# Own output tiles for the second batch in the last stage of a three-stage kernel, the last one stored in two halves

## The chip, the cores and the metric

One Trainium2 chip; the program runs on 1 core. The metric is the device time of one execution in microseconds (us). The engines are named as the profile names them: PE is TensorE's matmul, PEld its weight load, DVE VectorE, ACT ScalarE, POOL GpSimd, SP SyncE, whose queue issues the DMAs of this stage. TensorE's granted clock is 1.00 at 2.4 GHz and 0.50 at 1.2 GHz.

## The reference, cut to what matters

Three layers follow one another: an attention with bucketed masks, a mixture of experts in which every token goes to one expert, and a mixture of attention heads. The last one is what the change touches (two batches, S = 768 rows, D = 512 columns, E = 4 experts, Hd = 64):

```
logits = x @ w_gate                        # top 2 of 4 experts, softmax over the two
for e in range(E):
    q, k, v = x @ wq[e], x @ wk[e], x @ wv[e]
    scores = scale * (q @ k.T), causal mask, softmax -> a
    ye = a @ v @ wo[e]
    out += w[token, e] * ye                # w is 0 for an expert that was not chosen
```

## The kernel before

The kernel has three stages; the last is the class StageC. It takes two experts together as a unit u = (b, pp) with b the batch and pp the pair, so there are four units, and it cuts the 768 rows into halves h of 384 and into six tiles i of 128 (tile i belongs to half i // 3). For each unit it projects q and k, takes scores, exponentials and the causal mask, sums with the values (av), and divides and gates (gate, recip, norm).

The end of the stage is what matters here. norm(u, h, c0, c1) multiplies the gated sum by the reciprocal on DVE into a PSUM tile (can, line 1311), copies that with rounding on ACT (cah, or cxh for the last unit, line 1318), and takes the rest on DVE (cal or cxl, line 1319). For the last unit (1, 1) this is done for one row tile at a time. outp(b, i) then multiplies row tile i with the output weights: six matmuls of 512 columns into one PSUM tile cop (lines 1328 to 1330, three for each pair), then a copy out of PSUM and a DMA of 256 KB to the output (line 1342). For b = 0 the copy is one ACT instruction of 128x512 into a tile cos with two buffers (line 1341). For b = 1 it is an ACT instruction on the first 256 columns (line 1338) and a DVE instruction on the other 256 (line 1339).

Where the copy of b = 1 goes: self.ot is a tile of 2064 columns, a new one (tag w000h or w000l) whenever i is 0 or 3, and a row tile takes the part i % 3 of whichever self.ot is the latest. In the order below outp(1, 3) comes second, so that (1, 1) and (1, 4) both write the second part of the tile w000l, and (1, 2) and (1, 5) both its third part.

The order of all steps is written out by hand (ORDER_C), and each engine takes its instructions in that order; the costs and dependences in plan() give the list of steps and are only checked against it. The order ends, with the units' names left out where they are (1, 1): norm h=1 c=0; outp(1, 0); recip h=0 c=2; recip h=1 c=1; outp(0, 4); outp(1, 3); norm h=0 c=1; outp(0, 0); norm h=1 c=1; recip h=1 c=2; outp(1, 1); outp(1, 4); norm h=0 c=2; outp(0, 1); norm h=1 c=2; outp(1, 2); outp(1, 5). So outp(1, 1) needs norm h=0 c=1, outp(1, 4) needs norm h=1 c=1, outp(1, 2) needs norm h=0 c=2 and outp(1, 5) needs norm h=1 c=2.

The PSUM tiles can and cop (and others) share one ring of three buffers, in the order in which they are asked for:

```
def misc(self, shape, nm):
    return self.ps.tile(shape, F32, name=nm, tag="misc", bufs=3)
```

Counted along the order, cop of outp(1, 1) takes the buffer of can of norm h=0 c=1, and cop of outp(1, 2) that of can of norm h=0 c=2. The first matmul of a group so waits for the DVE instruction at line 1319 of that norm.

The tiles cu0, cu1, ck0, ck1, cq0 and cq1 hold what qk, low, twice, qcopy and mrow make of one unit (U, K and Q of its two experts), each with two buffers that the four units take in turn; their last readers are the score matmuls at lines 1256 and 1257. One more pair of instructions bears on the argument: low (line 1198, DVE) subtracts from partitions 64 to 127 of a PSUM tile cqp into the tile cl, and twice (line 1203, ACT) then copies the same partitions of that PSUM tile into another place (ck, partitions 0 to 63), so that the second needs no result of the first.

Of the kernel before, what the change touches and what calls it, by code (L numbers as in the profile page):

```python
# [8 lines left out]
F32 = mybir.dt.float32  # L9
# [8 lines left out]
B, H, S, D = 2, 8, 768, 64  # L18
DM = H * D
NP = H // 2  # L20
NKT = S // 128
# [11 lines left out]
WN = 2064  # L33
# [994 lines left out]
class StageC:  # L1028
# [292 lines left out]
    def outp(self, b, i):  # L1321
        nc = self.nc
        wh, wl = (a[:, 1040:2064].rearrange("p (k n) -> p k n", k=2) for a in self.wt[1])
        p = self.misc([128, DM], "cop")
        c = slice(128 * i, 128 * i + 128)
        for pp in range(2):
            ah, al = self.o[b, pp]
            nc.tensor.matmul(p, ah[:, c], wh[:, pp, :], start=pp == 0, stop=False)  # L1328
            nc.tensor.matmul(p, ah[:, c], wl[:, pp, :], start=False, stop=False)
            nc.tensor.matmul(p, al[:, c], wh[:, pp, :], start=False, stop=pp == 1)  # L1330
        if b == 0:
            t = self.p.tile([128, DM], F32, name="cos", bufs=2)
        else:
            if i % 3 == 0:
                self.ot = self.rp.tile([128, WN], F32, name="cot", tag=f"w000{'hl'[i // 3]}")
            t = self.ot[:, DM * (i % 3):DM * (i % 3) + DM]
        if b:
            nc.scalar.copy(t[:, :DM // 2], p[:, :DM // 2])
            nc.vector.tensor_copy(t[:, DM // 2:], p[:, DM // 2:])
        else:  # L1340
            nc.scalar.copy(t, p)
        nc.sync.dma_start(self.out[b, c], t)

    def plan(self):
        pl = Plan(dict(misc=3, sc=3, av=2))
# [4 lines left out]
        def add(name, *a, ops, deps=(), **kw):  # L1350
            pl.add((name, *a), lambda: getattr(self, name)(*a), ops, deps, **kw)
# [5 lines left out]
        for b in range(B):  # L1357
            for i in T:
                dep = [("trans", 0, j) for j in range(i // 3 * 3, i // 3 * 3 + 3)] if b else []
                if b:  # L1360
                    add("gather", b, i, ops=[("Pool", 1255)], deps=dep + [("busy",)], tail=2400)
                else:
                    add("came", b, i, ops=[(None, 1400 + 1255 * i)])
                add("scale", b, i, ops=[("ACT", 620) if b or i % 2 else ("DVE", 430, "p")], deps=[("gather" if b else "came", b, i)])
                dep = [("qk", u, x, i // 3) for u in us[:2] for x in X] + [("vproj", 0, i)] if b else []
                add("trans", b, i, ops=[("PE", 438 + (0 if b or i > 1 else (872, 436)[i])), ("ACT", 480), ("DVE", 605)], deps=[("scale", b, i)] + dep, bank="misc")
                add("vproj", b, i, ops=[("PE", 1440), ("ACT", 330)], deps=[("trans", b, i)], bank="misc")
                add("outp", b, i, ops=[("PE", 1390)] + ([("ACT", 290), ("DVE", 330)] if b else [("ACT", 490)]) + [("SP", 500)],
                    deps=[("norm", (b, 0), i // 3), ("norm", (1, 1), i // 3, i % 3, i % 3 + 1) if b else ("norm", (0, 1), i // 3)]
                    + ([("outp", b, i - 1)] if b and i % 3 else []), bank="misc", tail=2000)  # L1370
            add("gate1", b, ops=[("DVE", 1300, "p"), ("ACT", 200)], deps=[("vproj", b, i) for i in T])
            add("gate2", b, ops=[("DVE", 600, "p")], deps=[("gate1", b)])
            add("gate3", b, ops=[("PE", 110), ("DVE", 200), ("SP", 2500)], deps=[("gate2", b)] +
                ([("gate", u, h) for u in us[:2] for h in X] if b else []), bank="misc", tail=3500)
        for n, u in enumerate(us):
            b = u[0]
# [206 lines left out]
```

## Time and profile before

| | |
|---|---|
| median of 3 runs | 607.95 us (605.28 to 609.09) |
| the profiled execution | 608.14 us |
| its span, first to last instruction | 606.4 us |
| mean granted clock of TensorE | 0.987 |
| PE busy | 579.6 us (96%) |
| DVE, ACT, POOL busy | 443.1, 369.8, 252.1 us |

The span is what the trace covers; 1.74 us of the profiled execution's time lie outside it. Busy PE counts matmuls whose ends are modelled, so that one matmul is shown running into the next: the distance of their starts tells the pace.

### The profile page before, as it was taken

The page shows a single profiled execution, that of the slowest core. Times are in us where ns is not written, and L with a number is a line of the kernel's source. Part 1 is how long each engine was busy: PE and PEld are TensorE (multiplying, and loading weights), DVE is VectorE, ACT ScalarE, POOL GpSimd, SP SyncE. Part 2 cuts the span into 40 slices and gives each one's busy share as a digit, 9 for nine tenths or more (in the row PEclk, how much of TensorE's full clock was granted, in tenths as well). Part 3 has the DMA queues.
Part 4 walks back from the last instruction along what each step waited for, and adds up shares of the span by engine and source line. Part 5 has one row for each costly group of instructions (what it writes and reads, how often), then busy time and mean ns, then how long its engine had stood idle before and what let it go on. Part 6 is the DMA issues. An engine that isn't in the chain of part 4 may idle for free. (4 is left out here: it accounts for less than half of the span.)

```text
span 606.4 us, 9769 instructions
## 1 busy us (share of the span) xinstructions
PE 579.6 (96%) x3537; PEld 448.8 (74%) x3537; DVE 443.1 (73%) x853; ACT 369.8 (61%) x676; POOL 252.1 (42%) x256
## 2 busy tenths in 40 slices
PE   8999989999899999899999999999989999998995
PEld 3556657767576675798898998997969878787573
DVE  6699888988889798756656776755444576787872
ACT  4999878989695476154545545544537565554541
POOL 7696577686767784620000000000044024653840
PEclk8999999999999999899999999999999999999998
DMA  8535347265425415247656757665555010210222
GB/s 230 206 130 174 119 151 261 75 225 157 166 62 174 120 56 183 89 138 250 242 176 248 243 198 242 220 233 174 177 166 155 18 28 15 66 27 2 54 105 104
DMA packets 53718, 88.81 MB, mean 146 GB/s; under 512 B 3860, under 2 KB 26512, under 8 KB 53408
## 3 DMA queue, kind: packets, MB, share of 16 engines
q1 hardware_dynamic: 51712, 81.78, 41.3%
q0 software_dynamic: 1952, 6.34, 3.3%
q8 instruction: 29, 0.48, 0.4%
q14 instruction: 25, 0.20, 0.1%
HBM read 66.18 MB, written 20.26 MB: 143 GB/s over the span
## 5 line engine op out<-in xcount | busy, mean ns | idle before, releaser
L320 POOL TENSOR_TENSOR acc<-acc,pt 128x768 f32<-128x768 f32 x56 | 110.6, 1977 | 43.0 <-ACT pt L298 40.6
L274 DVE TENSOR_REDUCE m<-mp 128x1 f32<-128x384 f32 x192 | 96.4, 548 | 10.0 <-PE mp L273 9.2
L298 ACT ACTIVATE pt<-sc 128x384 f32<-128x384 f32 x192 | 85.5, 486 | 24.1 <-PE sc L297 21.1
L1079 POOL DMA_INDIRECT xg<-ys,slot x12 | 12.2, 1018 | 193.4 <-DVE wl L1049 185.7
L850 DVE TENSOR_TENSOR wlo<-wraw,whi 128x1024 fp32r<-128x1024 f32 x64 | 76.3, 1231 | 12.3 <-ACT whi L849 12.2
L307 PE MATMUL av<-pt,vt 128*64 128x385 f32 (+1 forms) x384 | 70.7, 493 | 0.0
L273 PE MATMUL mp<-km,qm 128*128 128x384 f32 x192 | 65.3, 379 | 5.4 <-DVE m L274 3.6
L849 ACT ACTIVATE whi<-wraw 128x1024 fp32r<-128x1024 f32 x64 | 64.4, 1053 | 9.0 <-DMA wraw<-in_w_dram 5.3
L295 PE MATMUL sc<-qm,km 128*128 128x384 f32 x192 | 67.6, 352 | 1.2 <-ACT pt L298 0.6
L297 PE MATMUL sc<-q,k 128*128 128x384 f32 x192 | 64.6, 336 | 0.0
L889 PE MATMUL hp<-xth,whi 128*128 128x256 f32 x224 | 63.0, 281 | 1.7 <-PEq L1017 1.7
L890 PE MATMUL hp<-xtl,whi 128*128 128x256 f32 x224 | 62.9, 281 | 0.0
L891 PE MATMUL hp<-xth,wlo 128*128 128x256 f32 x224 | 62.8, 280 | 0.0
L273 PEld LDWEIGHTS mp<-km,qm 128*128 128x128 f32 x192 | 35.6, 192 | 25.1 <-DVE m L274 10.6
L907 PE MATMUL yp<-whi,hh 128*128 128x512 f32 x128 | 51.5, 402 | 0.0
L908 PE MATMUL yp<-wlo,hh 128*128 128x512 f32 x128 | 50.4, 393 | 0.0
L909 PE MATMUL yp<-whi,hl 128*128 128x512 f32 x128 | 50.3, 393 | 0.0
L307 PEld LDWEIGHTS av<-pt,vt 128*64 128x64 f32 x384 | 25.4, 136 | 32.1 <-issue 28.8
L894 ACT ACTIVATE hh<-hp 128x512 fp32r<-128x512 f32 x32 | 19.1, 598 | 45.0 <-PE hp L891 44.9
L1281 POOL TENSOR_TENSOR cp<-cp,cp 128x384 f32<-128x384 f32 (+2 forms) x50 | 39.5, 812 | 17.0 <-PE cav L1273 16.1
L889 PEld LDWEIGHTS hp<-xth,whi 128*128 128x128 f32 x224 | 42.1, 188 | 2.4 <-issue 2.1
L895 DVE SCALAR_TENSOR_TENSOR hl<-hp,hh 128x512 fp32r<-128x512 f32 x32 | 22.0, 688 | 28.4 <-ACT hh L894 28.4
(263 smaller groups left out, 1387.6 us busy)
## 6 DMA issues: line engine op xcount, KB each, us to landing
wraw<-in_w_dram SPq DMA_DIRECT2D x32, 1024.0 KB
xs<-zt SPq DMA_DIRECT2D x13, 512.0 KB
x<-in_k_dram SPq DMA_DIRECT2D x14, 384.0 KB
x<-in_q_dram SPq DMA_DIRECT2D x14, 384.0 KB
xsb<-xs SPq DMA_DIRECT2D x7, 512.0 KB
ys<-ysb SPq DMA_DIRECT2D x7, 512.0 KB
vt<-in_v_dram SPq DMA_DIRECT2D x8, 384.0 KB
xp<-in_q_dram SPq DMA_DIRECT2D x7, 384.0 KB
```

Source lines behind the costliest of these rows:

```text
L273: nc.tensor.matmul(mp, QM[i][:, o:o + 128], KM[i][:, h * S + c * HS:h * S + (c + 1) * HS], start=True, stop=True)
L274: nc.vector.tensor_reduce(s["m"][:, qh, h, t, c:c + 1], mp, axis=AX.X, op=ALU.max)
L295: nc.tensor.matmul(sc, KM[i][:, h * S + kt * 128:h * S + kt * 128 + 128], QM[i][:, (2 * qh + h) * HS:(2 * qh + h + 1) * HS], start=True, s ...
L297: nc.tensor.matmul(sc, K1[i][:, h, ks], Q1[i][:, h, qs], start=False, stop=True)
L298: nc.scalar.activation(PT[(u * 12 + x) % NPB][:, h, :HS], sc, AF.Exp, scale=SCALE)
L307: nc.tensor.matmul(s["av", qh][64 * h:64 * h + 64, :HS + 1 - qh], s["v"][:, h, kt, :], P[:, h, :HS + 1 - qh], start=kt == 0, stop=kt == NK ...
L320: (nc.vector if u == NU - 1 else nc.gpsimd).tensor_add(s["acc", qh], p, P)
L849: nc.scalar.activation(hi[:, s], r[:, s], AF.Copy)
L850: nc.vector.tensor_sub(lo[:, s], r[:, s], hi[:, s].bitcast(F32))
L889: nc.tensor.matmul(p[:, f2, :], hi, xh[:, k, :], start=k == 0, stop=False)
L890: nc.tensor.matmul(p[:, f2, :], hi, xl[:, k, :], start=False, stop=False)
L891: nc.tensor.matmul(p[:, f2, :], lo, xh[:, k, :], start=False, stop=k == 3)
```

## The change

In the second batch each output row tile gets a tile of its own: the tags cu0, cu1, ck0, ck1, cq0 and cq1 are each asked for once more (i = 0 to 5), and the first 512 of their 768 columns are used. For i = 0 to 4 the copy is one ACT instruction of 128x512, as in the first batch. For i = 5 ACT copies the first 256 columns into the own tile and DVE the other 256 into a further tile (tag w000h), and each half has its own store of 128 KB; SP issues them one after the other. The cost entries of plan() follow; the order of the steps is the same. DVE so loses five copies, ACT's five copies are twice as wide, and SP issues one DMA more.

```diff
+        homes = ("cu0", "cu1", "ck0", "ck1", "cq0", "cq1")
         if b == 0:
             t = self.p.tile([128, DM], F32, name="cos", bufs=2)
         else:
-            if i % 3 == 0:
-                self.ot = self.rp.tile([128, WN], F32, name="cot", tag=f"w000{'hl'[i // 3]}")
-            t = self.ot[:, DM * (i % 3):DM * (i % 3) + DM]
-        if b:
-            nc.scalar.copy(t[:, :DM // 2], p[:, :DM // 2])
-            nc.vector.tensor_copy(t[:, DM // 2:], p[:, DM // 2:])
-        else:
+            t = self.p.tile([128, S], F32, name=homes[i], bufs=2)[:, :DM]
+        if b == 0 or i < NKT - 1:
             nc.scalar.copy(t, p)
-        nc.sync.dma_start(self.out[b, c], t)
+            nc.sync.dma_start(self.out[b, c], t)
+            return
+        t2 = self.rp.tile([128, WN], F32, name="cot", tag="w000h")[:, :DM // 2]
+        n = DM // 2
+        nc.scalar.copy(t[:, :n], p[:, :n])
+        nc.vector.tensor_copy(t2, p[:, n:])
+        nc.sync.dma_start(self.out[b, c, :n], t[:, :n])
+        nc.sync.dma_start(self.out[b, c, n:], t2)
...
-                add("outp", b, i, ops=[("PE", 1390)] + ([("ACT", 290), ("DVE", 330)] if b else [("ACT", 490)]) + [("SP", 500)],
+                add("outp", b, i, ops=[("PE", 1390)] + ([("ACT", 290), ("DVE", 330)] if b and i == NKT - 1 else [("ACT", 590)]) + [("SP", 500)],
```

## Rows read from the trace of the kernel before

**Rows 1.** The waits of 575 to 606.4 us: total us, times, longest.
```profile
DVE cot L1339 <- ACT cot L1338: 7.8, 5, 2.5
ACT cot L1338 <- DMA out_dram<-cot: 5.2, 2, 2.6
PE cop L1328 <- DVE cxl L1319: 2.4, 2, 1.9
```

**Rows 2.** The chain that ended last, 580 to 606.4 us: start, us, what.
```profile
593.13 2.01 DMA out_dram<-cot
...
597.46 0.23 PE cop L1329
...
598.32 0.43 PE cop L1329
...
600.07 2.00 DMA out_dram<-cot
...
602.57 0.42 DVE cot L1339
```

**Rows 3.** Timeline, 587 to 591 us, around TensorE's first stop.
```profile
587.13 1.75 DVE L1300 RECIPROCAL cr<-cr 128x128 f32<-128x128 f32 x2
588.05 0.33 SPq L1342 DMA_DIRECT2D out_dram<-cos  x1
588.79 0.37 ACT L1338 COPY cot<-cop 128x256 f32<-128x256 f32 x1 [0.77 <-PE cop L1330]
589.54 0.29 DVE L1311 TENSOR_TENSOR can<-ca,cr 128x128 f32<-128x128 f32 x1
589.74 0.40 PE L1330 MATMUL cop<-wh,cal 128*128 128x512 f32 x1
589.86 0.28 ACT L1318 ACTIVATE cxh<-can 128x128 fp32r<-128x128 f32 x1 [0.70 <-DVE can L1311]
590.61 0.47 PE L1328 MATMUL cop<-wh,cah 128*128 128x512 f32 x1 [0.47 <-DVE cxl L1319]
```

**Rows 4.** Timeline, 593 to 597.5 us, around its second stop.
```profile
593.23 0.40 PE L1330 MATMUL cop<-wh,cxl 128*128 128x512 f32 x1
594.62 0.40 PE L1330 MATMUL cop<-wh,cal 128*128 128x512 f32 x1
595.24 0.37 ACT L1338 COPY cot<-cop 128x256 f32<-128x256 f32 x1 [2.59 <-DMA out_dram<-cot]
595.64 0.42 DVE L1339 COPY cot<-cop 128x256 f32<-128x256 f32 x1 [2.54 <-ACT cot L1338]
596.31 0.28 ACT L1318 ACTIVATE cxh<-can 128x128 fp32r<-128x128 f32 x1 [0.69 <-DVE can L1311]
596.96 0.50 PE L1328 MATMUL cop<-wh,cah 128*128 128x512 f32 x1 [1.95 <-DVE cxl L1319]
597.30 0.39 PE L1329 MATMUL cop<-wl,cah 128*128 128x512 f32 x1
```

**Rows 5.** Busy time by stretch: PE, PEld, DVE, ACT, POOL, PEclk, DMA share, GB/s.
```profile
594.40:597.00 2.60, 0.65 (x4) 0.23 (x2) 1.01 (x4) 1.07 (x3) 0.00 (x0) 1.00 0.12 44
597.80:601.20 3.40, 3.40 (x10) 2.54 (x8) 0.42 (x1) 0.37 (x1) 0.00 (x0) 0.50 0.29 110
603.80:604.00 0.20, 0.00 (x0) 0.00 (x0) 0.00 (x0) 0.00 (x0) 0.00 (x0) 1.00 0.65 246
604.40:604.60 0.20, 0.00 (x0) 0.00 (x0) 0.00 (x0) 0.00 (x0) 0.00 (x0) 1.00 0.74 277
```

**Rows 6.** Timeline, 600.5 to 603 us, the last row tile.
```profile
601.10 0.46 PE L1330 MATMUL cop<-wh,cxl 128*128 128x512 f32 x1
602.17 0.37 ACT L1338 COPY cot<-cop 128x256 f32<-128x256 f32 x1 [2.58 <-DMA out_dram<-cot]
```

**Rows 7.** All instructions of lines 1341, 1342, 1256 and 1257: ns min/median/max, first and last start.
```profile
L1341 ACT COPY cos<-cop x6: 579/586/588, 579.3 to 596.5; 128x512 f32<-128x512 f32 x6
L1342 SPq DMA_DIRECT2D out_dram<-cot x6: 332/332/333, 587.2 to 603.0; - x6
L1256 PE MATMUL csc<-cu,ck x36: 219/344/449, 539.9 to 579.1; 128*128 128x384 f32 x20, 128*128 128x256 f32 x8, 128*128 128x128 f32 x8
L1257 PE MATMUL csc<-cq,cl x36: 273/335/347, 540.2 to 579.2; 65*128 65x384 f32 x20, 65*128 65x256 f32 x8, 65*128 65x128 f32 x8
```

**Rows 8.** Whom ACT waited for at line 1203 (us, times), a copy from PSUM.
```profile
  DVE cl L1198: 5.2, 8
```

## The prediction

> **What bounds the kernel now.** I read the end of the last stage first, since the change touches nothing ahead of it. The list of waits of the last 31 us [rows 1] shows three that belong together: ACT's copies waited 5.2 us for stores of the output tile, in two waits; DVE's copies waited 7.8 us for ACT's copies; and TensorE waited 2.4 us for DVE's rounding rest. The chain that ended last [rows 2] shows how they hang together: it runs twice through the 2.0 us flight of a store of cot. These are the two places at which a part of a tile is written again: outp(1, 4) takes the part that outp(1, 1) has just sent to a store, outp(1, 5) that of outp(1, 2). The reader is to see in the timeline what an ACT copy that waits for a store does to the rest [rows 4]: it begins at 595.24, DVE's half of the copy stands behind it until 595.64, the norm's instructions for the next row tile stand behind that on both engines (cxh at 596.31), and TensorE, whose last group started its last matmul at 594.62, goes on only at 596.96. After this stop its granted clock is 0.50 (1.2 GHz) from 597.8 to 601.2, having been 1.00 in the stretch with the stop [rows 5], and the starts of its matmuls, 0.23 us apart before, are 0.43 apart [rows 2]. A first, shorter stop of TensorE ends at 590.61 [rows 3]. Then the last row tile's copy waits for a store, until 602.17 [rows 6].
>
> **The change, part by part.** I follow TensorE's start times and shift them.
>
> *First stop.* Before, the product of norm h=0 c=1 stood on DVE at 589.54 behind DVE's half of the copy of outp(1, 3), and cxh followed on ACT at 589.86 [rows 3]. Now DVE has only the two reciprocals ahead of that product; they end at 588.88 at the latest, so it is done by 588.88 + 0.29 = 589.17. ACT is the later one: its copy starts at 588.79 as before, but takes 0.59 (the 128x512 copy of line 1341) [rows 7], so cxh begins at 589.38. From cxh to the first matmul it took 590.61 - 589.86 = 0.75 us here and 596.96 - 596.31 = 0.65 us at the second stop [rows 3, 4]; with 0.7 TensorE goes on at 590.08 in place of 590.61. It can't before 589.74 + 0.23 = 589.97. Gain 0.5, bounds 0.3 and 0.64.
>
> *Second stop.* outp(1, 4) starts its last matmul at 593.23 before [rows 4], now at 592.73, and ends it 0.40 later at 593.13. ACT's copy (no store to wait for) takes 593.15 to 593.74, cxh follows, and 0.7 later, at 594.44, outp(1, 2) may start. TensorE would be free for it at 594.62 + 0.23 - 0.5 = 594.35. So 0.1 of the stop is left: ACT's wide copy, queued ahead of cxh, is what is late next, by a hair, and behind it TensorE's own pace. Against 596.96 this is 2.5 earlier, 2.0 of it from this step; bounds 1.9 and 2.1. DVE's product is not the late one here: only one reciprocal (half of the 1.75 us pair) [rows 3] stands ahead of it.
>
> *Clock.* From the second to the last of the twelve matmuls after the stop the starts ran from 597.30 to 601.10, 3.80 us [rows 4, 6]; at 0.23 these ten steps take 2.3. With no stop above 0.1 us I expect the clock to stay at 1.00: gain 1.5. It is the least certain term, since another execution may have its low stretch elsewhere: bounds 0 and 1.5. I take 1.5, because the profiled execution lies within 0.2 us of the median of the runs.
>
> *Last wait.* The last matmul ends at 601.56 and the copy could start 0.02 later, but starts at 602.17 [rows 6]: 0.6 gained. Its tile is now its own.
>
> *Copy and store of the last row tile.* Before, counted from the start of ACT's copy: DVE starts at 0.40, ends at 0.82, the store is issued at 0.86 (603.03), takes 2.0 to land, and 1.37 later the span ends (606.40). Now the first half's store is issued at 0.41 and holds SP for 0.33 [rows 7]; the second half's depends on whether DVE may read the PSUM tile beside ACT. The nearest row is a pair that needs nothing of each other but reads one PSUM tile: ACT at line 1203 waited 8 times for DVE's line 1198 [rows 8]. So I take the two halves as one after the other: the second store is issued at 0.86 as before. If they run together it is issued at 0.41 + 0.33 = 0.74, so this decides 0.12 us only. In the Trainium skill, PSUM — Partial Sum Buffer (section PSUM bank collisions raise a hardware error) says that two engines must not access one bank of the same partitions at once, reads included; the row agrees. By that rule the halves are serial and the sum is as I have it.
>
> The second store moves half the bytes. The whole one moved its data from 603.8 to 604.6, 0.8 us at up to a full DMA share [rows 5]; half of that is 0.4 by bytes, and 0.8 if each of the 128 shorter rows costs what a long one does. The first half is gone from the engines by then or shares them for a moment. Gain 0.4 by bytes with serial halves, 0.54 with parallel ones, 0 if rows count; I take 0.3. A rule speaks against this part: in the Trainium skill, DMA: Bandwidth & Descriptors (Rules for kernel authors) says of two transfers to disjoint partition halves that they serialise on the same sixteen engines and aren't worth it. These are halves of columns, and no row of this trace has such a pair. By that rule the 0.3 would be nothing, and the sum 4.6.
>
> *What costs nothing.* ACT's five wide copies take 0.22 more each (0.59 against 0.37); where they stand ahead of cxh this is counted above, elsewhere ACT idles (0.77 and 2.59 us ahead of copies) [rows 3, 4]. Without that cover it would be 1.1. DVE loses five copies of 0.42. SP's additional issue lies behind the last copy and is counted. PSUM buffers come free sooner, one copy of 0.59 against two halves that took 0.82. The new tiles' buffers were last read by score matmuls that started by 579.2 [rows 7], over 6 us ahead of the first store at 587.2; nothing is left to wait for.
>
> *Sum.* 0.5 + 2.0 + 1.5 + 0.6 + 0.3 = 4.9 us. The span goes from 606.4 to 601.5; with the 1.74 outside it the profiled execution's 608.14 becomes 603.2. From the median of 607.95 it is 603.05. I say 603.1, 0.8% faster.
>
> **The rivals.**
> *The clock falls anyway*, or one of the norms is late enough on ACT for a stop of some tenths of a microsecond and a low stretch after it: the 1.5 us are not gained, 604.6. For it: the first copy-to-cxh queue leaves 0.1 in two places. Against it: the first stop of 0.47 us [rows 3] was followed by no low stretch.
> *The change doesn't do what it says:* the stops stay, because each copy waits for something else that comes at the same time. The plainest form is a wait for the store issued just ahead. From the store at 588.05, a link is 2.01 flight, 0.59 copy and 0.04 to the issue, 2.64: the store of outp(1, 3) at 590.69, of outp(0, 0) 0.59 later, of outp(1, 1) at 593.92, of outp(1, 4) at 596.56, of outp(0, 1) at 597.43 (behind cxh), of outp(1, 2) at 600.07, of the first half at 602.49, of the second 0.47 later, landed at 604.97; with 1.37 and 1.74 that is 608.1, no change. Against it: the copy of outp(1, 3) started at 588.79, with the store of 588.05 in flight [rows 3].
> *Slower* is the same mechanism with one more link, at the last row tile: the second half's copy also waits for the first half's store (2.01 + 0.42 + 0.04 from 602.49), issued at 604.96, landed at 606.97, 610.1. It decides the sign: up to the first half such waits only use up the gain; this last one puts 2 us on top. For it: the half stores are new and no row shows a pair. Against it: separate tiles, and the row of 588.79 again.
>
> **How the numbers follow.** All steps as told: 0.78. The clock or a new stop takes 1.5: 0.12. No change: 0.06. Slower: 0.04. By the bounds the forecast's gain lies between 2.8 (0.3 + 1.9 + 0 + 0.6 + 0) and 5.4 (0.64 + 2.1 + 1.5 + 0.6 + 0.54), times of 602.6 to 605.2 from the median; the runs of before lay 2.7 below and 1.1 above theirs, part of which a median of some runs takes out. The range is 601.0 to 605.8; the no-change and slower cases are outside it. A measurement of this kernel tells about 1% from no change, so 601.87 is the border to faster: the forecast lies 1.2 us above it, which the spread of runs crosses about one time in five. Faster 0.19, within 1% 0.76, slower 0.05.
>
> **What would show it.** In the changed kernel's waits no ACT copy waits for a store of an output tile; TensorE's groups follow at 0.23 us from 590.1 to about 597.4 with no stop above 0.2 us; the granted clock stays at 1.00 until then; the last matmul ends about 4.1 us earlier and the span 4.9 earlier; the second half's DVE copy starts when ACT's ends. The prediction is wrong if ACT's wide copy leaves cxh so late that a stop and a low clock come back, if a copy waits for the home tile's earlier user, or if the two half stores land later than one whole store did.

## The result and the profile after

The changed kernel takes 604.41 us (median of 16 runs, 601.08 to 607.87), the kernel before in its 16 runs 608.47 us (604.34 to 612.27). The ratio is 0.9913 with an interval of 0.9891 to 0.9935: 0.9% faster, about 5.3 us (4.0 to 6.6 by the interval), inside the 1% border, and inside the range of the prediction. The two medians themselves lie 4.06 us apart, at the lower end of that. The ratios here are of runs in the chip's fast state, which leaves out one of the ten runs of e1 (637.08 us, at a granted clock of 0.847).

The span of the profiled execution is 603.0 us, 3.4 less than before, and this number must not be read as the gain. All that is changed lies behind the first matmul of outp(1, 0). That started at 584.31 us before and at 586.13 in the changed kernel, 1.8 later, in code that is the same. So I measure everything from this matmul on and call it the tail: 606.40 - 584.31 = 22.09 us before, 603.0 - 586.13 = 16.87 after. The gain is 5.22 us, and the ratio of the runs (608.47 x 0.0087 = 5.3) agrees with it. The tail of the kernel before starts with this matmul, and two of its later events are used below, the second matmul of outp(1, 1) and the copy of outp(1, 2):

```profile
584.31 0.50 PE L1328 MATMUL cop<-wh,cah 128*128 128x512 f32 x1
...
590.91 0.39 PE L1329 MATMUL cop<-wl,cah 128*128 128x512 f32 x1
...
599.21 0.37 ACT L1338 COPY cot<-cop 128x256 f32<-128x256 f32 x1 [1.78 <-PE cop L1330]
```

The waits of the changed kernel from 575 us to the end (total us, times, longest), those that answer to [rows 1]:

```profile
DVE cxl L1319 <- ACT cxh L1318: 5.3, 6, 1.5
...
DVE cot L1343 <- ACT cq L1342: 2.1, 1, 2.1
...
PEld cop L1328 <- DVE cxl L1319: 0.5, 2, 0.2
```

No ACT copy waits for a store any more, and TensorE's two waits for the norms (0.5 and 1.95 us in [rows 3, 4]) have become two of 0.2 us at the weight load. What now stands first, DVE waiting for cxh, is ACT's wide copy queued ahead of cxh; of TensorE's time it costs no more than those two tenths, and the matmuls themselves lose 0.06 to 0.07 us at each place (0.29 to 0.30 from the first start to the second in place of 0.23). The timeline of the changed kernel at these two places and at the end (lines 1337, 1338 are the copy and store of all but the last row tile; 1342 to 1345 are those of the last):

```profile
586.13 0.50 PE L1328 MATMUL cop<-wh,cah 128*128 128x512 f32 x1
...
590.60 0.59 ACT L1337 COPY ck<-cop 128x512 f32<-128x512 f32 x1 [0.76 <-PE cop L1330]
...
591.09 0.28 ACT L1318 ACTIVATE cxh<-can 128x128 fp32r<-128x128 f32 x1
...
591.55 0.40 PE L1330 MATMUL cop<-wh,cal 128*128 128x512 f32 x1
591.78 0.46 PE L1328 MATMUL cop<-wh,cah 128*128 128x512 f32 x1
...
592.08 0.39 PE L1329 MATMUL cop<-wl,cah 128*128 128x512 f32 x1
...
594.83 0.59 ACT L1337 COPY cq<-cop 128x512 f32<-128x512 f32 x1 [0.79 <-PE cop L1330]
...
595.31 0.28 ACT L1318 ACTIVATE cxh<-can 128x128 fp32r<-128x128 f32 x1
...
595.78 0.40 PE L1330 MATMUL cop<-wh,cal 128*128 128x512 f32 x1
596.02 0.46 PE L1328 MATMUL cop<-wh,cah 128*128 128x512 f32 x1
...
596.31 0.39 PE L1329 MATMUL cop<-wl,cah 128*128 128x512 f32 x1
...
598.63 0.39 PE L1330 MATMUL cop<-wh,cxl 128*128 128x512 f32 x1
599.06 0.37 ACT L1342 COPY cq<-cop 128x256 f32<-128x256 f32 x1 [0.80 <-PE cop L1330]
599.46 0.33 SPq L1344 DMA_DIRECT2D out_dram<-cq  x1
599.47 0.42 DVE L1343 COPY cot<-cop 128x256 f32<-128x256 f32 x1 [2.11 <-ACT cq L1342]
599.92 0.35 SPq L1345 DMA_DIRECT2D out_dram<-cot  x1
```

The reader is to see that ACT goes from a copy straight to cxh, that the first matmul of outp(1, 1) and that of outp(1, 2) follow the one ahead at the usual 0.23 us (591.55 to 591.78, 595.78 to 596.02) and the second ones at 0.29 to 0.30, so that no stop is left, and that at the end DVE's half still starts when ACT's half ends, though they now write different tiles. Busy time by stretch, with the granted clock in the column ahead of the last two (columns as in [rows 5]): in the stretch of the last twelve matmuls it is 1.00 where it was 0.50 before, and the two half stores, issued at 599.46 and 599.92, move their data one after the other, with a dip at 600.6 to 600.8 between them.

```profile
596.00:597.80 1.80, 1.80 (x9) 1.49 (x9) 0.41 (x2) 0.89 (x3) 0.00 (x0) 1.00 0.42 163
597.80:598.60 0.80, 0.80 (x5) 0.66 (x4) 0.00 (x0) 0.46 (x1) 0.00 (x0) 1.00 0.77 289
...
600.20:600.40 0.20, 0.00 (x0) 0.00 (x0) 0.00 (x0) 0.00 (x0) 0.00 (x0) 1.00 0.41 148
600.40:600.60 0.20, 0.00 (x0) 0.00 (x0) 0.00 (x0) 0.00 (x0) 0.00 (x0) 1.00 1.06 379
600.60:600.80 0.20, 0.00 (x0) 0.00 (x0) 0.00 (x0) 0.00 (x0) 0.00 (x0) 1.00 0.46 149
600.80:601.00 0.20, 0.00 (x0) 0.00 (x0) 0.00 (x0) 0.00 (x0) 0.00 (x0) 1.00 0.85 297
601.00:601.20 0.20, 0.00 (x0) 0.00 (x0) 0.00 (x0) 0.00 (x0) 0.00 (x0) 1.00 0.90 312
```

### The profile page after: what moved, and what is told of

It reads as the page before. It is cut to its first block, busy times and chain, and to the rows that moved or that the text cites. A ratio compares the mean times of both kernels' runs of the same rounds, so it can differ in the third digit from the quotient of the medians.

```text
span 603.0 us, 9763 instructions
## 1 busy us (share of the span) xinstructions
PE 578.1 (96%) x3537; PEld 447.4 (74%) x3537; DVE 440.2 (73%) x848; ACT 370.9 (62%) x676; POOL 252.5 (42%) x256
## 5 line engine op out<-in xcount | busy, mean ns | idle before, releaser
L890 PEld LDWEIGHTS hp<-xtl,whi 128*128 128x128 f32 x224 | 42.1, 188 | 0.2
```

The costliest lines, as they stand in the source:

```text
L890: nc.tensor.matmul(p[:, f2, :], hi, xl[:, k, :], start=False, stop=False)
```

## The experiments

All tails are from the profiled execution of each kernel, from the first matmul of outp(1, 0) to the end of the span. "Last copy to end" goes from the start of the last ACT copy.

| kernel | starts, us | tail, us | last copy to end, us | ratio to before, timed |
|---|---|---|---|---|
| before | 584.31 | 22.09 | 4.23 | |
| changed | 586.13 | 16.87 | 3.94 | 0.9913 (0.9891 to 0.9935) |
| e1_own_parts | 584.75 | 18.45 | 4.29 | 0.9957 (0.9919 to 0.9994) |
| e2_act_alone | 582.49 | 19.61 | 4.01 | 0.9953 (0.9921 to 0.9984) |
| e3_last_whole | 581.75 | 16.95 | 4.01 | |
| e4_fill_stop | 582.36 | 21.54 | 4.22 | 0.9992 (0.9958 to 1.0025) |
| e5_last_in_halves | 586.17 | 16.43 | 3.45 | 0.9924 (0.9893 to 0.9955) |
| e6_last_384_128 | 584.04 | 16.56 | 3.33 | |
| e7_own_parts_act | 583.55 | 16.95 | 4.01 | |
| e8_before_2 | 586.44 | 22.06 | 4.23 | |
| e9_before_3 | 584.77 | 22.03 | 4.26 | |
| e10_fill_stop_2 | 585.74 | 21.56 | 4.25 | |

Each tail is of one execution. The three of the kernel before agree within 0.06 us and the two with the stop filled within 0.02, while the starts spread over 2.1 us in the three of before and 4.7 in all twelve. That is why tails are compared and not single times. The ends of the spans are given to 0.1 us, so that differences of tails below 0.1 us tell little. The six kernels below the first row that have no ratio were not timed beyond their one profiled execution.

**Parts of one's own, halves kept (e1_own_parts).** Only the shared parts are taken away:

```diff
-            if i % 3 == 0:
-                self.ot = self.rp.tile([128, WN], F32, name="cot", tag=f"w000{'hl'[i // 3]}")
-            t = self.ot[:, DM * (i % 3):DM * (i % 3) + DM]
+            if i == 0:
+                self.ot = {}
+            if i % 3 == 0:
+                self.ot[i // 3] = self.rp.tile([128, WN], F32, name="cot", tag=f"w000{'hl'[i // 3]}")
+            t = self.ot[i // 3][:, DM * (i % 3):DM * (i % 3) + DM]
```

> The kernel before, with its halves on ACT and DVE kept, but each row tile of the second batch in a part of its own (two tiles of three parts, held by half). The tail, from the first matmul of outp(1, 0) to the end of the span, was 22.1 us before and 16.9 after. My theory (two row tiles sharing a part are the cause of most of it): no ACT copy waits for a store, the second stop of TensorE shrinks from 1.95 us to about 0.5 (DVE's half is still queued ahead of the norm), the first stop stays at 0.47, the clock stays at 1.00, the last copy's wait is gone: 1.55 + 1.5 + 0.6 = 3.6 us off the tail, 18.4 us. Rival (taking the copies off DVE is the cause): the tail stays above 21. Rival (a tile waits for the stores of its other parts too): ACT copies still wait for stores and the tail stays near 22.

The tail is 18.45 us, 3.6 shorter, as expected. The timeline of TensorE shows both stops:

```profile
591.04 0.47 PE L1328 MATMUL cop<-wh,cah 128*128 128x512 f32 x1 [0.47 <-DVE cxl L1319]
595.83 0.50 PE L1328 MATMUL cop<-wh,cah 128*128 128x512 f32 x1 [0.38 <-DVE cxl L1319]
```

The first is as it was (0.47), the second has shrunk from 1.95 to 0.38; no ACT copy waits for a store, and the clock is 1.00 from 584 to 600 us. Taking away the parts that two row tiles shared so gives 3.6 of the 5.2 us by itself. Whether a tile would also wait for stores of its other parts isn't told apart by this run: here those stores had all landed in time.

**ACT alone, parts shared (e2_act_alone).** The other half of the change: the copy of the second batch is the one ACT instruction `nc.scalar.copy(t, p)`, into the parts of before.

> The kernel before, with the copy of the second batch as one ACT instruction of 128x512, into the same parts as before, two of them used twice. My theory: the first stop of TensorE shrinks to 0.2 or less (0.5 us off); the copy of outp(1, 4) still waits for the store of outp(1, 1), now issued about 0.7 us earlier, and the stop behind it is still about 1.4 us; the last copy still waits for a store. Tail 20 to 21 us in place of 22.1, by whether the clock falls after the stop. Rival (ACT alone is the cause): the tail is near 17 and TensorE does not stop.

The tail is 19.61, a little better than the 20 to 21 expected. The first stop is gone, the second is 1.1 us where about 1.4 was expected:

```profile
592.52 0.58 ACT L1337 COPY cot<-cop 128x512 f32<-128x512 f32 x1 [2.12 <-DMA out_dram<-cot]
...
593.66 0.50 PE L1328 MATMUL cop<-wh,cah 128*128 128x512 f32 x1 [1.11 <-DVE cxl L1319]
...
598.09 0.58 ACT L1337 COPY cot<-cop 128x512 f32<-128x512 f32 x1 [2.14 <-DMA out_dram<-cot]
```

ACT's copies still wait 2.1 us for stores, twice. After this shorter stop the clock stayed at 1.00 to the last matmul, the better of the two cases expected, and the last copy to the end takes 4.01 in place of 4.23, which the expectation had left out. The two single edits give 3.64 and 2.48 us, together more than the 5.14 that both give at once: each of them already shortens the second stop and brings the clock back, in the one execution of each that was profiled.

**Both edits without the six tiles (e7_own_parts_act).** The parts of e1 with the copy of e2.

> The kernel before with its two output tiles of three parts kept and held by half (no two row tiles share a part), and the copy of the second batch as one ACT instruction of 128x512; the last row tile is whole. It joins the two single edits, each of which took a part of the gain. My theory (the six tiles of their own do nothing that a part of one's own doesn't): tail 16.9 to 17.0 us as with the last row tile whole in the changed kernel, with no stop above 0.25 us. Rival (a tile waits for the stores of its other parts, or the place of the tile counts): ACT copies wait for stores, tail 18 or more.

16.95, and no ACT copy waits for a store. The tiles taken from the units' tags do nothing that a part of one's own doesn't do.

**The last row tile whole (e3_last_whole).** In the changed kernel the condition `if b == 0 or i < NKT - 1:` becomes `if True:`.

> The changed kernel, with the last row tile treated as the five others: one ACT copy of 128x512 and one store of 256 KB. From the start of the last ACT copy to the end of the span it was 4.23 us before and 3.94 in the changed kernel. My theory (the two halves of the copy are serial, since both read one PSUM tile, so that the split saves little): copy 0.59, issue 0.04 later, 2.0 to land, 1.37 to the end: 4.0 us, a tail 0.06 longer than the changed kernel's 16.9. Rival (the smaller last store is what gains): 4.2 us or more.

16.95 against 16.87, and 4.01 against 3.94: the split of the last row tile is worth 0.07 us, about what the tails of one kernel differ by, so little or nothing (e2 and e7, whole too, also take 4.01 from the last copy to the end). Its second store does land sooner, but is issued 0.86 us after the start of the copy in place of 0.61, behind two serial half copies, and the two effects nearly cancel.

**The stop filled (e4_fill_stop, e10_fill_stop_2).** In the kernel before, nine matmuls into a free PSUM tile behind outp(0, 1):

```diff
         nc.sync.dma_start(self.out[b, c], t)
+        if (b, i) == (0, 1):
+            self.g["warm"](self.ps.tile([128, 512], F32, name="csc", bufs=3), 9)
```

> The kernel before, with nine matmuls of 512 columns that nobody reads put behind outp(0, 1), where TensorE stops for 1.95 us; all copies, parts and stores as before. My theory (1.5 us of the gain is the low clock after the stop): the granted clock stays at 1.00 to the end of the tail, the starts of the last twelve matmuls are 0.23 us apart, and the tail is 1.4 us shorter, 20.7, less what the ninth matmul runs over (0.2 at most); the last copy still waits for a store, so that some of the 1.4 may be taken back by that wait (copy of outp(1, 2), store, 2.0 us). Rival (the low stretch would come anyway, by time and not by the stop): the clock falls all the same and the tail stays at 22.1 or more.

> The kernel with nine matmuls that nobody reads in TensorE's second stop, profiled once more. Theory (no stop, no low stretch): clock 1.00 throughout the tail and 21.5 us again. Rival (low stretches come by time): a stretch at 0.50 in the tail.

The clock stayed at 1.00 to the last matmul in both executions, and the last twelve matmuls ran at 0.23 us (those of e4 from 595.01 to 597.67 us, those of e10 from 598.39 to 601.05). Busy time by stretch, one of e4 and two of e10, columns as in [rows 5]:

```profile
596.00:598.00 2.00, 2.00 (x9) 1.32 (x8) 0.42 (x1) 0.37 (x1) 0.00 (x0) 1.00 0.33 124
...
598.00:600.00 2.00, 2.00 (x9) 1.34 (x8) 0.79 (x3) 0.77 (x3) 0.00 (x0) 1.00 0.67 253
600.00:602.00 2.00, 1.44 (x7) 0.83 (x5) 0.42 (x1) 0.37 (x1) 0.00 (x0) 1.00 0.13 48
```

But the tail is 21.54 and 21.56, only 0.55 shorter, where the first expectation led with 20.7. ACT's last copies in e4 show where the rest went:

```profile
596.72 0.37 ACT L1338 COPY cot<-cop 128x256 f32<-128x256 f32 x1 [1.24 <-PE cop L1330]
599.68 0.37 ACT L1338 COPY cot<-cop 128x256 f32<-128x256 f32 x1 [2.59 <-DMA out_dram<-cot]
```

The two lie 599.68 - 596.72 = 2.96 us apart, as before (602.17 and 599.21): the second waits for the store of the first, and what TensorE gained in between became a longer wait. Only the 0.54 by which the copy of outp(1, 2) came earlier (14.36 against 14.90 us from the start of the tail) is kept.

**The kernel before again (e8_before_2, e9_before_3).** No edit.

> The kernel before, unchanged, profiled once more, to see whether the low clock behind TensorE's second stop belongs to the kernel or to one execution. Theory (the stop of 1.95 us brings it each time): a stretch at a granted clock of 0.50 among the last twelve matmuls, tail 22.1 us within 0.2. Rival (it depends on where the execution's low stretches fall): clock 1.00 to the last matmul; then, by the run with the stop filled, the last copy's wait for the store takes most of it back, and the tail is 21.5.

> As the run before it: the same kernel and the same two expectations, a third execution.

Both have the low clock behind the stop: behind the fourth of the twelve matmuls their starts go from 0.23 to 0.43 us apart, as in the first profile. The granted clock in a stretch of e8 and in one of e9, then the chain of e8:

```profile
600.00:602.00 2.00, 2.00 (x7) 1.50 (x6) 0.29 (x1) 0.37 (x1) 0.00 (x0) 0.51 0.35 131
...
598.00:600.00 2.00, 2.00 (x7) 1.59 (x6) 0.22 (x2) 0.37 (x1) 0.00 (x0) 0.60 0.39 144
```

```profile
599.83 0.24 PE cop L1330
600.07 0.35 PE cop L1328
600.41 0.43 PE cop L1329
```

So with the stop of 1.95 us the low stretch came in three executions of three, and with the stop filled in none of two. The other seven profiles, whose longest stop here is 1.11 us, fit: in each of them the granted clock is 1.00 from 575 us to the last matmul.

**The last row tile in two PSUM tiles (e5_last_in_halves, e6_last_384_128).** The core of the edit of the changed kernel; in e6 the cut is at column 384.

```diff
+        if (b, i) == (1, NKT - 1):
+            n = DM // 2
+            for y in range(2):
+                p = self.misc([128, n], "cop")
+                cc = slice(n * y, n * y + n)
+                for pp in range(2):
+                    ah, al = self.o[b, pp]
+                    nc.tensor.matmul(p, ah[:, c], wh[:, pp, cc], start=pp == 0, stop=False)
+                    nc.tensor.matmul(p, ah[:, c], wl[:, pp, cc], start=False, stop=False)
+                    nc.tensor.matmul(p, al[:, c], wh[:, pp, cc], start=False, stop=pp == 1)
+                t = self.p.tile([128, S], F32, name=("cq1", "cq0")[y], bufs=2)[:, :n]
+                if y:
+                    nc.scalar.copy(t, p)
+                else:
+                    nc.vector.tensor_copy(t, p)
+                nc.sync.dma_start(self.out[b, c, cc], t)
+            return
```

> The changed kernel, but the last row tile is computed in two PSUM tiles of 256 columns, one after the other (twelve matmuls of 256 columns in place of six of 512); DVE copies the first while TensorE works on the second, ACT the second; each half has its own store of 128 KB. My theory (in the changed kernel DVE's half waits for ACT's because both read one PSUM tile; TensorE's pace for 256 columns is half of that for 512, about 0.12 us): after the last matmul there is one half copy of 0.37 and a store of 128 KB, its issue 0.41 after the start of the copy in place of 0.86, so the tail is 16.4 in place of 16.9 us. Rival (the halves are serial for another reason, or TensorE's weight loads set the pace of narrow matmuls, 0.19 each): the gain of 0.45 is lost to 0.5 to 0.9 more on TensorE, tail 17 us or more.

> As the run with the last row tile in two PSUM tiles of 256 columns, but cut at column 384: the part after the last matmul is a copy of 128 columns and a store of 64 KB. My theory: the copy is 0.1 shorter (0.28 for 128 columns against 0.37) and the store lands up to 0.2 sooner if the bytes count, so 0.1 to 0.3 us off, tail 16.1 to 16.3; if rows count and not bytes, 0.1. Rival (TensorE's weight loads set the pace of narrow matmuls): the six matmuls of 128 columns take 0.19 each in place of 0.06, 0.4 us or more lost, tail 16.6 or more.

e5 gives 16.43, as expected: DVE's half is copied while TensorE works on the other, and 3.45 us are left from the start of the last copy. It is the shortest tail of all, 0.44 below the changed kernel. Its measured ratio to before, 0.9924, can't be told from the changed kernel's 0.9913; the intervals are several times wider than 0.44 us. e6 leaves 3.33, 0.12 less, but its tail is 16.56: the theory had TensorE's matmuls of 128 columns at 0.06 us and the rival at 0.19; they take 0.11. From the first start to the last the twelve matmuls take 1.56 us (595.40 to 596.96) against 1.30 in e5 (597.54 to 598.84), which is more than the copy and the store give back. The chain of e6, columns start, us, what:

```profile
596.44 0.18 PE cop L1334
596.61 0.06 PE cop L1332
596.67 0.11 PE cop L1333
596.78 0.11 PE cop L1334
```

Matmuls of 384 columns follow at 0.18 us and of 128 columns at 0.11, as those of 256 do in e5 (0.12). A matmul of 128 columns so costs nearly what one of 256 does, and this cut gains nothing over e5.

## Why the prediction was right

From the start of the tail, with 584.31 taken off the times of before and 586.13 off those after:

| step | event | before | after | step, measured | predicted |
|---|---|---|---|---|---|
| first stop | second matmul of outp(1, 1) | 6.60 | 5.95 | 0.65 | 0.5 (0.3 to 0.64) |
| second stop | second matmul of outp(1, 2) | 12.99 | 10.18 | 2.16 | 2.0 (1.9 to 2.1) |
| clock | last matmul | 16.79 | 12.50 | 1.48 | 1.5 (0 to 1.5) |
| last wait | last ACT copy | 17.86 | 12.93 | 0.64 | 0.6 |
| copy and store | end of the span | 22.09 | 16.87 | 0.29 | 0.3 (0 to 0.54) |
| sum | | | | 5.22 | 4.9 |

Each row is the difference of before and after, less that of the row above. (The event at 6.60 is the matmul at 590.91 us of the timeline before.)

**The stops.** Both terms were a little small, mainly for one reason. I had cxh start when ACT's copy ends, 0.59 after its start. The profile after has 590.60 to 591.09 and 594.83 to 595.31: ACT starts the next instruction 0.48 to 0.49 us after the start of a copy of 0.59. The trace of before had such a pair already, which I overlooked:

```profile
590.22 0.59 ACT L1341 COPY cos<-cop 128x512 f32<-128x512 f32 x1
...
590.70 0.28 ACT L1318 ACTIVATE cxh<-can 128x128 fp32r<-128x128 f32 x1
```

The tenth that I had left of the second stop so shrinks to what TensorE loses in restarting, 0.06 from one start to the next (0.29 in place of 0.23 us), and the first stop goes to the limit that I had given.

**The clock.** The size was right (1.48), and that it comes from the stop is shown by the filled stop and by the repeated profiles. But the prediction treated it as a term of its own, and that it isn't: with the shared parts kept, the same clock was worth 0.55. The 1.5 are only gained together with the last wait. The rival that the clock falls anyway is refuted by the profile after and by all others without the long stop, and my lower bound of 0 was too careful: in the three executions of before the low stretch came behind the same matmul each time.

**The last wait** has 0.6 as told. **Copy and store** came out as the 0.3 that I took, which was in part luck: I had chosen it between 0 and 0.54. Against before, with the second store issued 0.86 us after the start of the copy as told, the half-sized last store saves 0.29. Each half moved its data in 0.4 to 0.5 us where the whole needed 0.8, so the time went by bytes and not by rows; why 0.29 and not 0.4 came of it is not shown. Against one ACT copy and one store, which any version without the split has, it saves 0.07, if anything. That the halves of one PSUM tile are copied one after the other by ACT and DVE was foreseen from [rows 8]: the half at 599.47 has its own destination and shares only the PSUM tile with the one at 599.06, and starts 0.04 after that ends. The rule of the Trainium skill, PSUM — Partial Sum Buffer (PSUM bank collisions raise a hardware error), that two engines must not access one bank of the same partitions at once, agrees with the order in which the program runs; that the chip would do harm otherwise no run here shows. The rule of the Trainium skill, DMA: Bandwidth & Descriptors (Rules for kernel authors), that two transfers to disjoint partition halves aren't worth it, is close to what e3 measured for halves of columns: 0.07 us. With halves that TensorE delivers one after the other (e5) the split is worth 0.44 more: DVE's half is copied from 598.45 to 598.87, before the last copy starts at 599.15, and the last store is issued 0.40 us after that start in place of 0.86.

**The rivals.** The wait for the store issued just ahead, and with it the slower case, is refuted by the waits after: no copy waits for any store.

**The time.** The forecast of 603.1 was made from a median of 607.95 of three runs. The sixteen runs have 608.47, half a microsecond more; the gain was forecast as 4.9 and is 5.2 to 5.3. With that gain the median would have been 603.2; it was 604.41. The 1.2 us between them I put down to the spread of starts, not to the change, as the tail has no room for it; no run shows it.

## What to carry to other kernels

In this kernel a wait for a buffer was paid three times: by the engine that waits, by all that is queued behind it in order on that and the next engine, and by TensorE's clock after the longer stop; look for tiles that are written again while their store is in flight, above all where an index picks a part of "the latest" tile. Terms that lie in one chain don't add up one by one: filling the stop alone gave 0.55 us, because the next wait took what it had won. And when starts vary by more than the edit is worth, measure from an event just ahead of the edit in the trace.

## What the hardware showed that I had not expected

- The low clock follows the stop and not the time: after stops of TensorE of 1.95 us the granted clock fell to 0.50 within the next twelve matmuls in three executions of three, and in neither of two executions with the stop filled; after a stop of 1.11 us (e2, one execution) it stayed at 1.00, as after those of 0.47 and 0.38 us (e1).
- A good part of the spread of starts arises in the first 26 us, in code that all twelve profiles share, and it goes with the clock. The first exponential (line 298) starts at 22.4 to 23.3 us in six of them, which have a granted clock of 0.86 to 1.00 in the first 25 us, and at 24.9 to 26.2 in the other six, with 0.73 to 0.76. The first profile of before is of the first kind (22.8, 0.86), e8, of the same kernel, of the second (25.3, 0.76), and so is that of the changed kernel (26.2, 0.74), whose tail starts later than in the first profile of before. The cause wasn't tried.
- Two half stores of 128 KB issued 0.46 us apart moved their data one after the other, in 0.4 to 0.5 us each, the second done at about 601.2 us; the whole one of 256 KB needed 0.8 [rows 5].
